# An attention and two-stage MLP kernel: TensorE's order fixed from the second pair's transposes on, and scores of pairs 2 to 4 on four array squares

## The chip, the cores and the metric

The kernel runs on one core of one Trainium2 chip. A core has TensorE (PE; its weight loads are shown as PEld), VectorE (DVE), ScalarE (ACT), GpSimd (POOL) and SyncE (SP), which here issues every DMA. The metric is the time of one execution on the device in microseconds; lower is better.

## What is computed

Attention with a window of 128 keys and a bias that falls with distance, over 4 batches of 8 heads, 576 positions, 64 values a head; then two MLPs on the 2304 tokens.

```python
scores = scale * q @ k.T                       # q, k, v: (4, 8, 576, 64)
scores = where(0 <= i - j < 128, scores + bias, -1e9)
attn   = softmax(scores)
x      = (attn @ v) laid out as (2304, 512)
a, b   = x @ w1, x @ w2                        # 512 -> 1024
x      = (a * b) @ w3 @ w_out                  # 1024 -> 1024 -> 512
h      = x @ w_in                              # 512 -> 2048
out    = (h * clip(h + 3, 0, 6) / 6) @ w_out2  # 2048 -> 512
```

## The kernel before

**Pairs.** Heads are taken two at a time: 16 pairs, four to a batch. `products(n, part)` makes the scores of pair n (tile s, line 159), part 0 for query blocks 0 to 5 and part 1 for 6 to 8. A block has 64 queries against up to 192 keys. The two heads lie in the two halves of the partitions; each matmul uses one 64x64 square of the array. Without a swap only the two squares on the diagonal are used; for pairs above 4 a copy with the halves exchanged (`other`, tiles qo and ko) lets odd blocks use the other two squares. `scores` reduces on DVE (line 173) and takes the exponential on ACT (line 178); `normalize` forms reciprocals on DVE (lines 183 and 184) and scales on POOL (line 187). `pt(n, g)` transposes the probabilities on TensorE (line 214), 24 matmuls for each g, and copies them out on ACT and DVE (tile th, line 220). `pv(n)` multiplies by the values (tile X, line 241) and moves the result out (tile xf, lines 248 and 249), and `x_parts` splits it into x. Each float32 matmul leaves two records in the trace: 24 and 12 for the two parts of the scores, 48 for one pt, 44 for one pv.

**Banks.** All score, transpose and value tiles share three double banks of PSUM, p0 to p2 (`bank2`, line 140): pair n in role r takes p((n+r)%3). So scores of part 1 of pair 1 stand where pv(0) has left its first half, and scores of part 0 of pair 2 where those stood.

**Weights.** w3 and w_out come as 64-bit words. `unpack` makes float32 of them (lines 66, 67, 71), `split` a high and a low part (lines 77 and 78), and `mm3` multiplies in three matmuls (lines 53 to 55). W = w3 @ w_out is made ahead in rows i = 0 to 7 (`w_half(i, half)`, tile wps): rows 0 and 1 in plain float32 (line 393), rows 2 to 7 as two halves of 12 matmuls each. A row needs its `w3_unit(i)`. `more` loads the next raw block into one of three buffers, when that buffer's last user is done. `w12_unit(f)` does the same for w1 and w2.

**Order.** Tile's planner gives each engine a fixed order from its own estimate of times, earlier lines of the program first. `in_order(True, ...)` keeps an instruction behind the one that precedes it in the program on the same engine. Before the first matmul of ab (x times w1 and w2) `written[0]` is false: scores and values stay together but for their first matmul, transposes and `w_half` float. `attn_slot(6n+s)` spreads pair n over six slots, between which `do_work` puts the weight units; `GATE` holds the last halves of W behind pair 3. From the first ab on, `written[0]` is true: `block(k)` puts `gap` pieces of ab or y, 12 matmuls each, between the steps of a pair. Pairs 0 to 3, and the scores of pair 4 (made here in part), come before the first ab; pairs 4 to 7 fill block 0.

**Buffers.** `place(n)` says which of two q, k, v buffers pair n uses: it alternates up to pair 3, after which all use the first. q and k of pair n+2 are loaded behind pt of pair n (`loads`). The exchanged copy had one buffer, in pool a3, which was opened after the raw pools close.

Of the kernel before, what the change touches and what calls it, by code (L numbers as in the profile page):

```python
# [9 lines left out]
F32 = mybir.dt.float32  # L10
# [8 lines left out]
P = 128  # L19
# [4 lines left out]
def tile_attention_moe_moe2(ctx: ExitStack, tc: tile.TileContext, qT, kT, vm, vt, wo, w3, w12, w2x, out):  # L24
# [82 lines left out]
    HB = (slice(0, D), slice(D, 2 * D))  # L107
    qw, kw, vw = [], [], []
    for i, pool in enumerate((a1, a2)):
        qw.append(pool.tile([P, S], F32, name=f"qw{i}"))  # L110
        kw.append(pool.tile([P, S], F32, name=f"kw{i}"))
        vw.append(pool.tile([P, NC, P], F32, name=f"vw{i}"))
# [6 lines left out]
    def load_hp(n, names):  # L119
        for nm in names:  # L120
            if nm == "v":
                nc.sync.dma_start(out=vw[place(n)][:, 0 : NC - 1, :], in_=vm[n])
                nc.sync.dma_start(out=vw[place(n)][D:P, NC - 1, :], in_=vt[n])
            else:
                r, src = (qw, qT) if nm == "q" else (kw, kT)
                nc.sync.dma_start(out=r[place(n)], in_=src[n])
                if n > NP:
                    for h in range(2):
                        nc.sync.dma_start(out=other[nm][HB[h], :], in_=src[n][HB[1 - h], :])

    other = {}
    prob = {}
# [16 lines left out]
    def products(n, part):  # L149

        t = bank2(n, part, f"s_{n}_{part}")
        for a in range(0, len(PARTS[part]), 2):
            for h in range(2):
                for i in PARTS[part][a : a + 2]:
                    swap = n > NP and i % 2 == 1
                    r = 1 - h if swap else h
                    q, k = (other["q"], other["k"]) if swap else (qw[place(n)], kw[place(n)])
                    o = t[:, i % 2, COL[i] : COL[i] + width(i)]
# [140 lines left out]

    def pair_steps(n):  # L300

        if n == NP:
            yield from (lambda s=s: attn_slot(SLOTS * n + s) for s in (2, 3, 4))
        else:

            def first():
                for part in range(2):
                    products(n, part)
                for js in ((0, 1, 2), (3, 4, 5), (6, 7, 8)):
                    scores(n, js)  # L310
                    normalize(n, js)

            def second():
                pt(n, 0)
                loads(n, "q")
                pt(n, 1)
                loads(n, "k")

            yield first
            yield second  # L320
        yield lambda: pv(n)

# [61 lines left out]
    def w_half(i, half):  # L384
# [6 lines left out]
        for m in range(half * KH, (half + 1) * KH):  # L391
            if i < WHOLE:
                nc.tensor.matmul(ps[:, 0:DM], w3v[i][:, m, :], wof[m], start=m == 0, stop=m == KF - 1)
                continue
            hi, lo = w3v[i]
            mm3(ps[:, 0:DM], hi[:, m, :], lo[:, m, :], *wov[m], m == 0, m == KF - 1)
        if half == 1:
# [36 lines left out]

    work = []
    for i in range(KF):
        work += [("w3", i), ("h", i, 0), ("h", i, 1)]
    head = work.index(("w3", 2))
    work[:head] = [
        ("w3", 0), ("wo", 0), ("wo", 1), ("h", 0, 0), ("w3", 1), ("h", 1, 0),  # L440
        ("wo", 2), ("wo", 3), ("h", 0, 1), ("h", 1, 1),
    ]
    a = work.index(("h", WHOLE - 1, 1)) + 1
    work[a:a] = [("ws", i) for i in range(KH)]
    for f in range(W12_EARLY):
        work.insert(work.index(("h", KH + 1 + f, 1)) + 1 if f < KH - 1 else len(work), ("w12", f))
    FILL = {0: 2, 1: 4, 2: 6, 3: 8, 4: 10}
    nslot = SLOTS * NP + 2

    GATE = {  # L450
        (KF - 2, 1): ("pt", NP - 1, 1),
        (KF - 1, 0): ("x", NP - 1, 1), (KF - 1, 1): ("x", NP - 1, 1),
    }

    def do_work(w):
        if w[0] == "h":

            gate = GATE.get(w[1:])
            with tc.issue_after(last_pe[gate].ins) if gate in last_pe else nullcontext():
                w_half(w[1], w[2])  # L460
        else:
# [4 lines left out]
    wi = 0  # L466
    end = work.index(("h", KF - 2, 0))
    for s in range(nslot):
        attn_slot(s)

        upto = FILL[s] if s in FILL else FILL[4] + (s + 1 - len(FILL)) * (end - FILL[4]) // (SLOTS * NP - 2 - len(FILL))
        if s >= SLOTS * NP - 2:
            upto = work.index(("h", KF - 2, 1)) + 1
        if s >= SLOTS * NP:
            upto = len(work)
        while wi < min(upto, len(work)):
            do_work(work[wi])
            wi += 1


    raw_ctx2.close()
    raw_ctx.close()
    a2_ctx.close()
    a3 = apool_ctx.enter_context(tc.tile_pool(name="a3", bufs=1, side="right"))
    for nm in "qk":
        other[nm] = a3.tile([P, S], F32, name=f"{nm}o")
    gp = p1.enter_context(tc.tile_pool(name="gp", bufs=1))
# [169 lines left out]
    def block(k):  # L657

        work = pieces(k)
        for n in range(NP * (k + 1), NP * (k + 2)):  # L660
            steps = list(pair_steps(n))
            gaps = (3, 1, 1, 1) if n == NP else (4, 1, 1) if n == NP + 1 else (3, 1, 1)
            for step, gap in zip(steps, gaps):
                step()
                for _ in range(gap):
                    yield next(work)
# [272 lines left out]
```

## Time and profile before

| | us |
|---|---|
| median of 3 runs | 845.68 (845.66 to 845.82) |
| the profiled execution | 845.8 |
| its span (first to last instruction) | 844.0 |
| TensorE busy | 824.2 |
| DVE, ACT, POOL busy | 466.4, 378.4, 98.1 |
| first matmul of ab starts | 100.47 |

All times on the trace count from the start of the span. A row of the timeline gives start, duration, engine, line, operation, output<-inputs, shapes and a count of merged instructions; in square brackets stands the idle time of the engine before it and what ended it. Matmuls overlap, so the time that a group takes is the distance from its start to the next group's start, not the sum of durations.

### The profile page before, as it was taken

The numbers are of one execution on the slowest core, as the hardware profiler recorded it, in microseconds if no ns is written. First come the engines' busy times: TensorE is split into PE (matmuls) and PEld (weight loads), VectorE is DVE, ScalarE is ACT, GpSimd is POOL, SyncE is SP. The second block draws the span as 40 slices with busy tenths as digits, with TensorE's granted clock in tenths as the row PEclk, the third lists the DMA queues.
The fourth block names the chain that finished last, engine by engine and source line by source line (L and its number), as shares of the span: only waits on it lengthen the run. The fifth ranks groups of instructions, "written<-read, shape, count | busy, mean of one in ns | idle before, by whom it ended". The sixth has DMA issues, their size and how long they took to land.

```text
span 844.0 us, 15817 instructions
## 1 busy us (share of the span) xinstructions
PE 824.2 (98%) x6304; PEld 698.5 (83%) x6304; DVE 466.4 (55%) x1054; ACT 378.4 (45%) x820; POOL 98.1 (12%) x185
## 2 busy tenths in 40 slices
PE   5989999999999999999999999999999999999998
PEld 4567777888888788888899898998889889898886
DVE  5985477425452454246573877885543547443543
ACT  7765565525441445224352654555332335332333
POOL 3333303222231222300000000000000000000000
PEclk9989999999999999999999999999999999999999
DMA  9753543334332332316666589589855377455502
GB/s 352 284 217 100 162 137 102 99 100 114 95 91 73 104 81 62 125 64 237 261 194 239 229 333 363 160 303 390 326 196 215 138 274 293 189 208 203 188 1 75
DMA packets 42841, 155.62 MB, mean 184 GB/s; under 512 B 4880, under 2 KB 20240, under 8 KB 31504
## 3 DMA queue, kind: packets, MB, share of 16 engines
q1 hardware_dynamic: 42768, 154.62, 51.2%
q8 instruction: 49, 0.80, 0.4%
q14 instruction: 24, 0.20, 0.1%
HBM read 118.55 MB, written 36.04 MB: 183 GB/s over the span
## 4 chain that ended last, share of the span: by engine, by line
PE 91%; DVE 4%; ACT 2%; DMA 1%; issue 1%; POOL 0%; SPq 0%; DVEq 0%; POOLq 0%
PE ab L53 8%; PE o L54 8%; PE o L55 8%; PE o L53 8%; PE ab L54 8%; PE ab L55 7%; PE h L53 7%; PE h L54 7%; PE h L55 7%; PE y L53 4%; PE y L54 4%; PE y L55 4%; PE s L159 3%; PE X L241 3%; PE pt L214 3%; DMA raww<-in_w_dram 1%
## 5 line engine op out<-in xcount | busy, mean ns | idle before, releaser
L53 PE MATMUL ab<-x,w12h 128*128 128x512 f32 (+1 forms) x320 | 121.3, 379 | 0.4 <-ACT asb L517 0.4
L54 PE MATMUL ab<-x,w12h 128*128 128x512 f32 (+1 forms) x320 | 118.1, 369 | 0.0
L55 PE MATMUL ab<-x,w12l 128*128 128x512 f32 (+1 forms) x320 | 117.9, 369 | 0.0
L53 PE MATMUL h<-yh,va 128*128 128x384 f32 x336 | 114.1, 340 | 0.2 <-DVE rl L748 0.2
L54 PE MATMUL h<-yl,va 128*128 128x384 f32 x336 | 113.3, 337 | 0.3 <-DVE yl L78 0.3
L55 PE MATMUL h<-yh,va 128*128 128x384 f32 x336 | 113.3, 337 | 0.0
L54 PE MATMUL o<-vo,g 128*128 128x512 f32 x288 | 113.2, 393 | 0.0
L53 PE MATMUL o<-vo,g 128*128 128x512 f32 x288 | 113.1, 393 | 0.0
L55 PE MATMUL o<-vo,g 128*128 128x512 f32 x288 | 87.2, 393 | 0.0
L187 POOL TENSOR_SCALAR pr<-pr,rc 128x192 f32<-128x192 f32 (+1 forms) x144 | 71.9, 519 | 131.5 <-ACT pr L178 79.1
L747 ACT ACTIVATE rl<-c,three 128x384 f32<-128x384 f32 x72 | 44.4, 617 | 79.5 <-DVE c L777 48.4
L53 PEld LDWEIGHTS ab<-x,w12h 128*128 128x128 f32 x320 | 60.4, 189 | 14.3 <-issue 2.0
L178 ACT ACTIVATE pr<-pr,mn 128x192 f32<-128x192 f32 (+1 forms) x144 | 61.3, 427 | 19.8 <-DVE mn L173 19.7
L55 PEld LDWEIGHTS ab<-x,w12l 128*128 128x128 f32 x320 | 60.4, 189 | 10.2
L53 PEld LDWEIGHTS h<-yh,va 128*128 128x128 f32 x336 | 63.1, 188 | 6.7 <-DVE rl L748 3.1
L54 PEld LDWEIGHTS ab<-x,w12h 128*128 128x128 f32 x320 | 60.4, 189 | 9.0
L54 PEld LDWEIGHTS h<-yl,va 128*128 128x128 f32 x336 | 63.1, 188 | 4.2 <-DVE yl L78 0.6
L55 PEld LDWEIGHTS h<-yh,va 128*128 128x128 f32 x336 | 63.1, 188 | 0.0
L55 PEld LDWEIGHTS o<-vo,g 128*128 128x128 f32 x288 | 53.9, 188 | 10.5 <-DVE g L78 0.3
L78 DVE TENSOR_TENSOR g<-rl,g 128x384 fp32r<-128x384 f32 x96 | 53.2, 555 | 16.8 <-ACT g L77 14.3
L53 PEld LDWEIGHTS o<-vo,g 128*128 128x128 f32 x288 | 54.1, 188 | 9.5 <-ACT g L77 0.2
L54 PEld LDWEIGHTS o<-vo,g 128*128 128x128 f32 x288 | 54.1, 188 | 9.3
(95 smaller groups left out, 1371.4 us busy)
## 6 DMA issues: line engine op xcount, KB each, us to landing
va<-vad SPq DMA_DIRECT2D x18, 1792.0 KB, 7.4
vo<-vod SPq DMA_DIRECT2D x18, 1024.0 KB, 9.5
raww<-in_w_dram SPq DMA_DIRECT2D x16, 1024.0 KB, 4.9
rawv<-in_w2x_dram SPq DMA_DIRECT2D x16, 1024.0 KB, 7.4
vad<-va SPq DMA_DIRECT2D x8, 1792.0 KB, 7.3
vod<-vo SPq DMA_DIRECT2D x8, 1024.0 KB, 10.9
yraw<-yT SPq DMA_DIRECT2D x21, 384.0 KB, 9.1
qw<-in_qT_dram SPq DMA_DIRECT2D x16, 288.0 KB, 3.9
```

Source lines behind the costliest of these rows:

```text
L53: in_order(pinned, nc.tensor.matmul(ps, lh, rh, start=first, stop=False, **kw))
L54: in_order(pinned, nc.tensor.matmul(ps, lh, rl, start=False, stop=False, **kw))
L55: in_order(pinned, nc.tensor.matmul(ps, ll, rh, start=False, stop=last, **kw))
L78: lo_eng.tensor_tensor(out=lo, in0=src, in1=f32(hi), op=ALU.subtract)
L159: in_order(written[0] or (a, h, i % 2) != (0, 0, 0), nc.tensor.matmul(o[HB[h], :], q[HB[r], i * D : (i + 1) * D], k[HB[r], (i + 1) * D - w ...
L178: nc.scalar.activation(o, o, AF.Exp, bias=mn[:, i : i + 1], scale=-1.0, accum_out=sm[:, i : i + 1])
L187: nc.gpsimd.tensor_scalar(out=o, in0=o, scalar1=rc[:, i : i + 1], scalar2=1.0, op0=ALU.mult, op1=ALU.mult)
L214: last_pe["pt", n, g] = in_order(written[0], nc.tensor.matmul(t[HB[c], h, o : o + D], prob[n, i][HB[h], (k - i + 2) * D : (k - i + 3) * D] ...
L241: last_pe["x", n, h] = in_order(written[0] or begun, nc.tensor.matmul(X[p][HB[h], a * D : b * D], vw[place(n)][HB[p], k // 2, HB[h]], pts[ ...
L747: nc.scalar.activation(rl, h, AF.Relu, bias=three[:, 0:1], scale=1.0)
```

## The change

- Exchanged copies `other` now exist in both places, in pools a1 and a2, and pool a3 is gone. They are loaded, as four more half-height DMAs for each pair, from pair 2 on instead of from pair 5 on; the scores of pairs 2, 3 and 4 swap their odd blocks as those of later pairs do.
- The slots run only to the end of pair 1's scores; behind them come the four `wo_split` and `w3_unit` 2 and 3, and `written[0]` becomes true there. From there every scores, pt, pv and `w_half` matmul up to ab is kept in program order. `GATE` and the slot schedule of the rest are gone.
- That order, with h(i,b) for half b of row i of W: h(2,0), scores(2,0); then for n = 1, 2, 3: half, pt(n) whole, half, pv(n), half, scores(n+1, 1), and for n below 3 half, scores(n+2, 0). That is twelve halves with a step of a pair between each two. `w3_unit(i+2)` stands ahead of row i, and `w12_unit` 0 to 2 behind rows 5 to 7.
- `normalize` of pair 4's last blocks comes ahead of block 0. In block 0, pair 4's two transposes stand together, and pairs 5 to 7 have two pieces between transposes and values instead of one.

```diff
--- before.py
+++ after.py
@@ -106,7 +106,10 @@
     W = {}
     HB = (slice(0, D), slice(D, 2 * D))
     qw, kw, vw = [], [], []
+    other = {}
     for i, pool in enumerate((a1, a2)):
+        for nm in "qk":
+            other[nm, i] = pool.tile([P, S], F32, name=f"{nm}o{i}")
         qw.append(pool.tile([P, S], F32, name=f"qw{i}"))
         kw.append(pool.tile([P, S], F32, name=f"kw{i}"))
         vw.append(pool.tile([P, NC, P], F32, name=f"vw{i}"))
@@ -124,11 +127,10 @@
             else:
                 r, src = (qw, qT) if nm == "q" else (kw, kT)
                 nc.sync.dma_start(out=r[place(n)], in_=src[n])
-                if n > NP:
+                if n > 1:
                     for h in range(2):
-                        nc.sync.dma_start(out=other[nm][HB[h], :], in_=src[n][HB[1 - h], :])
-
-    other = {}
+                        nc.sync.dma_start(out=other[nm, place(n)][HB[h], :], in_=src[n][HB[1 - h], :])
+
     prob = {}
     stat = {}
     pts = {}
@@ -152,9 +154,9 @@
         for a in range(0, len(PARTS[part]), 2):
             for h in range(2):
                 for i in PARTS[part][a : a + 2]:
-                    swap = n > NP and i % 2 == 1
+                    swap = n > 1 and i % 2 == 1
                     r = 1 - h if swap else h
-                    q, k = (other["q"], other["k"]) if swap else (qw[place(n)], kw[place(n)])
+                    q, k = (other["q", place(n)], other["k", place(n)]) if swap else (qw[place(n)], kw[place(n)])
                     o = t[:, i % 2, COL[i] : COL[i] + width(i)]
                     in_order(written[0] or (a, h, i % 2) != (0, 0, 0), nc.tensor.matmul(
                         o[HB[h], :], q[HB[r], i * D : (i + 1) * D], k[HB[r], (i + 1) * D - width(i) : (i + 1) * D],
@@ -297,28 +299,17 @@
             pt(n, s - 3)
             loads(n, "qk"[s - 3])
 
-    def pair_steps(n):
-
-        if n == NP:
-            yield from (lambda s=s: attn_slot(SLOTS * n + s) for s in (2, 3, 4))
-        else:
-
-            def first():
-                for part in range(2):
-                    products(n, part)
-                for js in ((0, 1, 2), (3, 4, 5), (6, 7, 8)):
-                    scores(n, js)
-                    normalize(n, js)
-
-            def second():
-                pt(n, 0)
-                loads(n, "q")
-                pt(n, 1)
-                loads(n, "k")
-
-            yield first
-            yield second
-        yield lambda: pv(n)
+    def first(n, part):
+        products(n, part)
+        for js in ((6, 7, 8),) if part else ((0, 1, 2), (3, 4, 5)):
+            scores(n, js)
+            normalize(n, js)
+
+    def second(n):
+        pt(n, 0)
+        loads(n, "q")
+        pt(n, 1)
+        loads(n, "k")
 
     flat = lambda t: t.rearrange("p a b -> p (a b)")
     KH = KF // 2
@@ -393,7 +384,7 @@
                 nc.tensor.matmul(ps[:, 0:DM], w3v[i][:, m, :], wof[m], start=m == 0, stop=m == KF - 1)
                 continue
             hi, lo = w3v[i]
-            mm3(ps[:, 0:DM], hi[:, m, :], lo[:, m, :], *wov[m], m == 0, m == KF - 1)
+            mm3(ps[:, 0:DM], hi[:, m, :], lo[:, m, :], *wov[m], m == 0, m == KF - 1, pinned=written[0])
         if half == 1:
             split(W["h"][:, i, :], W["l"][:, i, :], ps[:, 0:DM], nc.vector)
 
@@ -432,58 +423,63 @@
     load_wo(3)
     more()
 
-    work = []
-    for i in range(KF):
-        work += [("w3", i), ("h", i, 0), ("h", i, 1)]
-    head = work.index(("w3", 2))
-    work[:head] = [
+    work = [
         ("w3", 0), ("wo", 0), ("wo", 1), ("h", 0, 0), ("w3", 1), ("h", 1, 0),
         ("wo", 2), ("wo", 3), ("h", 0, 1), ("h", 1, 1),
     ]
-    a = work.index(("h", WHOLE - 1, 1)) + 1
-    work[a:a] = [("ws", i) for i in range(KH)]
-    for f in range(W12_EARLY):
-        work.insert(work.index(("h", KH + 1 + f, 1)) + 1 if f < KH - 1 else len(work), ("w12", f))
     FILL = {0: 2, 1: 4, 2: 6, 3: 8, 4: 10}
-    nslot = SLOTS * NP + 2
-
-    GATE = {
-        (KF - 2, 1): ("pt", NP - 1, 1),
-        (KF - 1, 0): ("x", NP - 1, 1), (KF - 1, 1): ("x", NP - 1, 1),
-    }
 
     def do_work(w):
         if w[0] == "h":
-
-            gate = GATE.get(w[1:])
-            with tc.issue_after(last_pe[gate].ins) if gate in last_pe else nullcontext():
-                w_half(w[1], w[2])
+            w_half(w[1], w[2])
         else:
             {"wo": wo_unit, "ws": wo_split, "w3": w3_unit, "w12": w12_unit}[w[0]](w[1])
             if w[0] in ("w3", "w12"):
                 more()
 
     wi = 0
-    end = work.index(("h", KF - 2, 0))
-    for s in range(nslot):
+    for s in range(SLOTS + 3):
         attn_slot(s)
-
-        upto = FILL[s] if s in FILL else FILL[4] + (s + 1 - len(FILL)) * (end - FILL[4]) // (SLOTS * NP - 2 - len(FILL))
-        if s >= SLOTS * NP - 2:
-            upto = work.index(("h", KF - 2, 1)) + 1
-        if s >= SLOTS * NP:
-            upto = len(work)
-        while wi < min(upto, len(work)):
+        while wi < FILL.get(s, len(work)):
             do_work(work[wi])
             wi += 1
-
+    for i in range(KH):
+        wo_split(i)
+    for i in range(WHOLE, WHOLE + 2):
+        do_work(("w3", i))
+    written[0] = True
+
+    def rows():
+        for i in range(WHOLE, KF):
+            if i + 2 < KF:
+                do_work(("w3", i + 2))
+            for half in range(2):
+                w_half(i, half)
+                if half and i > KH:
+                    do_work(("w12", i - KH - 1))
+                yield
+
+    fill = rows()
+    next(fill)
+    first(2, 0)
+    for n in range(1, NP):
+        next(fill)
+        second(n)
+        next(fill)
+        pv(n)
+        if n + 1 < NP:
+            load_hp(n + 2, "v")
+        next(fill)
+        first(n + 1, 1)
+        if n + 2 <= NP:
+            next(fill)
+            first(n + 2, 0)
+    for _ in fill:
+        pass
 
     raw_ctx2.close()
     raw_ctx.close()
     a2_ctx.close()
-    a3 = apool_ctx.enter_context(tc.tile_pool(name="a3", bufs=1, side="right"))
-    for nm in "qk":
-        other[nm] = a3.tile([P, S], F32, name=f"{nm}o")
     gp = p1.enter_context(tc.tile_pool(name="gp", bufs=1))
     sp = p1.enter_context(tc.tile_pool(name="sp", bufs=1))
 
@@ -658,10 +654,14 @@
 
         work = pieces(k)
         for n in range(NP * (k + 1), NP * (k + 2)):
-            steps = list(pair_steps(n))
-            gaps = (3, 1, 1, 1) if n == NP else (4, 1, 1) if n == NP + 1 else (3, 1, 1)
-            for step, gap in zip(steps, gaps):
-                step()
+            late = k == 0
+            if n > NP:
+                first(n, 0)
+                first(n, 1)
+            gaps = (3, 1, 1) if n == NP else (4, 2, 1) if n == NP + 1 else (3, 1 + late, 1)
+            for step, gap in zip((None, second, pv), gaps):
+                if step:
+                    step(n)
                 for _ in range(gap):
                     yield next(work)
         for w in work:
```

## Rows read from the trace of the kernel before

**Rows 1.** The page: busy time by engine, and the chain that ended last.

```profile
PE 824.2 (98%) x6304; PEld 698.5 (83%) x6304; DVE 466.4 (55%) x1054; ACT 378.4 (45%) x820; POOL 98.1 (12%) x185
...
PE 91%; DVE 4%; ACT 2%; DMA 1%; issue 1%; POOL 0%; SPq 0%; DVEq 0%; POOLq 0%
```

**Rows 2.** Windows, whole stretch: length, busy (instructions) by engine, clock, DMA, GB/s.

```profile
37.20:100.47 63.27, 59.14 (x673) 46.66 (x673) 43.08 (x111) 36.71 (x88) 19.88 (x31) 0.95 0.45 161
```

**Rows 3.** Waits of TensorE in 37 to 63 us: total, times, longest.

```profile
PE pt L214 <- POOL pr L187: 1.8, 2, 1.5
PE X L241 <- DVE th L220: 1.2, 1, 1.2
```

**Rows 4.** Windows as in group 2: before and during the clock's fall.

```profile
50.00:54.50 4.50, 1.44 (x33) 0.79 (x33) 4.05 (x8) 3.47 (x6) 2.75 (x3) 0.99 0.47 193
54.50:61.00 6.50, 6.50 (x32) 4.91 (x33) 5.17 (x18) 4.02 (x11) 1.17 (x1) 0.50 0.48 161
```

**Rows 5.** Timeline of TensorE: scores of one pair on two squares, then on four.

```profile
86.08 1.88 PE L159 MATMUL s<-kw,qw 64*64 64x64 f32 x24 [0.36 <-PE pt L214]
...
99.34 1.20 PE L159 MATMUL s<-kw,qw 64*64 64x192 f32 x12
100.47 0.50 PE L53 MATMUL ab<-x,w12h 128*128 128x512 f32 x1
...
120.92 0.27 PE L159 MATMUL s<-kw,qw 64*64 64x64 f32 x1
...
122.49 0.50 PE L53 MATMUL ab<-x,w12h 128*128 128x512 f32 x1
```

**Rows 6.** Timeline of TensorE: transposes, values and the matmuls behind them.

```profile
116.47 1.58 PE L241 MATMUL X<-th,vw 64*64 64x192 f32 x44
117.98 0.50 PE L53 MATMUL ab<-x,w12h 128*128 128x512 f32 x1
...
134.29 1.63 PE L214 MATMUL pt<-ident,pr 64*64 64x64 f32 x96
135.85 0.50 PE L53 MATMUL ab<-x,w12h 128*128 128x512 f32 x1
```

**Rows 7.** Timeline of TensorE and ACT about the first matmuls of this stage.

```profile
35.58 1.48 PE L241 MATMUL X<-th,vw 64*64 64x192 f32 x37
37.19 0.50 PE L53 MATMUL wps<-wovh,w3h 128*128 128x512 f32 x1
...
33.12 1.19 ACT L66 ACTIVATE raww<-raww 128x1024 f32<-128x1024 f32 x1 [0.43 <-DMA raww<-in_w_dram]
...
39.34 0.64 ACT L248 COPY xf<-X 128x576 f32<-128x576 f32 x1
```

**Rows 8.** Timeline of DVE and POOL between pair 1's last scores and transposes.

```profile
44.34 0.84 DVE L67 TENSOR_SCALAR raww<-raww 128x1024 int32<-128x1024 int32 x1 [0.87 <-DMA raww<-in_w_dram]
...
47.84 0.35 DVE L173 CUSTOM_DVE_ANT_0 pr<-s,rel 128x192 f32<-128x192 f32 x1
...
51.63 2.75 POOL L187 TENSOR_SCALAR pr<-pr,rc 128x192 f32<-128x192 f32 x3 [7.00 <-DVE rc L184]
...
63.72 1.23 POOL L187 TENSOR_SCALAR pr<-pr,rc 128x192 f32<-128x192 f32 x3 [0.79 <-DVE rc L184]
```

**Rows 9.** Timeline of TensorE and DVE: pair 5's values and a copy they awaited.

```profile
139.09 0.54 PE L241 MATMUL X<-th,vw 64*64 64x192 f32 x4 [0.23 <-DVE th L220]
140.70 1.54 PE L241 MATMUL X<-th,vw 64*64 64x192 f32 x40 [1.06 <-DVE th L220]
...
140.09 0.55 DVE L220 COPY th<-pt 128x384 f32<-128x384 f32 x1
```

**Rows 10.** DMA in 16 to 32 us (as group 2), and issues: size, landing.

```profile
16.00:32.00 16.00, 14.00 (x115) 6.50 (x116) 15.90 (x33) 14.06 (x25) 9.49 (x10) 0.97 0.99 405
...
qw<-in_qT_dram SPq DMA_DIRECT2D x16, 288.0 KB, 3.9
...
qo<-in_qT_dram SPq DMA_DIRECT2D x22, 144.0 KB, 3.4
```

## The prediction

> **What bounds the kernel now.** Read first the busy line and the chain: TensorE is busy 98% of the span and carries 91% of the chain [rows 1]. So a microsecond of TensorE time that goes away ahead of the end is a microsecond of the whole, unless a wait takes its place. Read next where TensorE is not at its best. Between the first matmul of W's row 2 at 37.19 us and the first of ab at 100.47 us, 63.3 us pass [rows 5, 7]; there DVE is busy for 43.1 us, ACT for 36.7 and POOL for 19.9 [rows 2], so no other engine fills the stage. The waits show 1.8 us for probabilities scaled on POOL and 1.2 us for a transpose's copy [rows 3], 3.0 us together, and a further 0.36 us ahead of scores [rows 5]. Behind the longest of these, after a stretch in which TensorE was busy 1.44 of 4.5 us, the granted clock is 0.50, the lower level of 1.2 GHz, for 6.5 us [rows 4]. Work done at half speed for 6.5 us costs 3.25 us. Last, read the length of like groups of matmuls: a pair's scores on two squares take 1.88 us (part 0) and 1.13 us (part 1, 99.34 to 100.47), 3.0 us together, and on four squares 1.57 us (120.92 to 122.49) [rows 5].
>
> **The change part by part.** It touches the stage from 37 to 100 us and block 0 behind it. I count the new stage from its parts, then check it against the old.
>
> *The written order.* From pair 1's last scores to ab TensorE now has one queue: twelve halves of W, scores of pairs 2 to 4, transposes and values of pairs 1 to 3, none of which can be overtaken. Twelve three-matmul products between other groups take 2.94 us (117.98 to 120.92: one piece of ab, the same twelve matmuls of 512 columns, drain included) [rows 5, 6]. So the halves take 12 x 2.94 = 35.3 us. Transposes of a pair take 1.56 us (134.29 to 135.85) and values 1.51 us (116.47 to 117.98) [rows 6], three times each 4.7 and 4.5 us. Scores of pairs 2 to 4 take 3 x 1.57 = 4.7 us, and pair 1's last part, still on two squares, 1.1 us [rows 5]. The sum is 50.3 us.
>
> *Its start.* Pair 1's last scores go into the bank that pair 0's values leave. Those end at 37.1, but ACT copied them out only at 39.34 to 39.98 us, and the old kernel filled that time with row 2 of W from 37.19 on [rows 7]. The new order puts these scores ahead of row 2, so TensorE may idle there. The earliest start is 37.1 + 0.64 for the copy and some 0.4 for the two hand-overs, 38.2; the latest that the rows speak for is 40.0. I take 40.0, as ACT's order ahead of it is not changed. Ab would then start at 90.3 us, without a further wait.
>
> *New waits.* In the written order the half behind a transpose is all that covers its copies on ACT and DVE. Block 0 already runs such an order, and there pair 5's values waited 0.23 and 1.06 us, since the second copy came at 140.09 us between weight units on DVE [rows 9]; pair 4's did not [rows 6]. So a wait of this kind costs 0 to 1.3 us for each of three pairs; I take one of them, 1.3 us, which gives 91.6 us. What stands queued behind such a wait is everything to ab. Scaled probabilities get 2.94 + 1 + 2.94, about 7 us of cover between a pair's last scores and its transposes; in the old stage three scalings took 1.23 us on a free POOL and 2.75 us at worst [rows 8], which that covers when DVE comes in time.
>
> *The check from the old side.* Of 63.3 us go the waits of 3.0 and 0.36, the clock's 3.25, and 3 x (3.0 - 1.57) = 4.3 us of scores: 10.9, which leaves 52.4. A gap of 40.0 - 37.2 = 2.8 us at the start and a wait of 1.3 us come in: 56.5, so ab starts at 93.7 us. The two counts give 91.6 and 93.7 us; their middle, 92.7 us, is 7.8 us before the old 100.47.
>
> *Block 0.* Pairs 5 to 7 have two pieces between transposes and values instead of one, 5.9 us in place of 2.94, so the 1.3 us that pair 5's values waited [rows 9] go. Pair 4's transposes stand together; this saves one change of form, between 0 and 0.3 us, counted at nothing. The piece taken for this comes from the tail of the same block: no work is added.
>
> *Loads.* Each of pairs 2, 3 and 4 brings four more DMAs of 144 KB, 0.59 MB, and SP issues all in order. For pairs 3 and 4 they stand beside loads of weights that are wanted some 15 us later in the new order than in the old: nothing. Pair 2's fall into 16 to 32 us, where the DMA engines are 0.99 busy at 405 GB/s [rows 10]: what is queued behind them, row 4 of w3, comes 0.59 MB / 405 GB/s = 1.5 us later. If a half-height load is slower by the byte, as its landing of 3.4 us for 144 KB beside 3.9 us for 288 KB [rows 10] would have it, 1.7 times as much, 2.5 us. Row 4 is wanted at about 57 us in the new order, so I count nothing; but ACT already waited 0.43 us for it at 33.12 [rows 7], and what ACT has queued behind is the copying that frees TensorE's banks. So this can cost 0 to 2.5 us at the start; I take 0 and keep the rest for a rival.
>
> *DVE, ACT and POOL* do the same operations as before, 43.1 us of DVE in a stage that shrinks to 55.5 us: a share of 78% instead of 68%. That is the load that it had in 50 to 61 us (9.2 of 11 us) or a little under [rows 4], and there it was late.
>
> *Sum.* The gain is 7.8 + 1.3 = 9.1 us. The profiled execution took 845.8 us with a span of 844.0, and agrees with the median of 845.68 to 0.1. Behind block 0 nothing is anchored to a fixed time; all moves forward. 845.7 - 9.1 = 836.6 us.
>
> **The rivals.**
>
> *A, the vector chain holds the order up once.* In the old stage DVE took pair 1's last score blocks only at 47.84 us, behind an unpacking of w3 that waited 0.87 us for its DMA at 44.34 [rows 8]; its order is planned with estimated times. If it does so again, scores of pair 2, which need that bank, stand until 48.7 where TensorE could start them at 40.0 + 1.1 + 2.9 = 44.0: 4.7 us. Then 1.0 for them, 2.9 for a half and 0.8 for half the transposes bring TensorE to 53.4, and the rest waits for POOL until 54.4 (51.63 + 2.75) [rows 8]: 1.0 us more. If the clock falls again, 3.25 us [rows 4]. Together 9.0: 845.6 us. Without the clock, and with half of the delay, 839.5. For it speaks that only the TensorE order is written, not DVE's; against it, that pair 1's scores now come ahead of row 2, so that the planner sees them ready earlier.
>
> *B, slower: the same at every pair.* Where the old order let TensorE take any ready half of W while it waited, the new one cannot. If DVE is late for pairs 2 and 3 as well, by the 1.3 us of the copies each [rows 9], A's 845.6 becomes 848.2 us. It decides from 9.1 us of new idle time on, and its place is the stage from 40 to 60 us. Against it speaks that DVE's weight work after 60 us is sparser: POOL's scalings are back at 1.23 us [rows 8].
>
> The Trainium skill ("SBUF — State Buffer", "SBUF: two separate sides") says that POOL and a DVE operation with two SBUF inputs hold a shared port in turn, each for its whole length, which speaks against packing both closer. The trace agrees in that the three scalings went from 1.23 to 2.75 us; by the rule they would be at 2.75 at every pair, which the 7 us of cover still hold, so that it only raises B.
>
> *C, the early queue.* Pair 2's four loads push ACT back as above: 2.5 us, 839.1 us. The row for it is the DMA share of 0.99; against it, that the half-height loads are issued behind the weights that are wanted first.
>
> *D, the swap brings nothing there.* Its 4.3 us stay: 840.9 us. The 1.57 us of pair 5 [rows 5] speak against it.
>
> **How the numbers follow.** Forecast 836.6 us, chance 0.60, with an own range of 832 to 840: down by a start at 38.2 (1.8) and no copy wait (1.3) and by the first count alone (1.0), up by two more copy waits (2.6). C 0.08, D 0.04. A 0.18, of which 0.05 within 0.2% of before (1.7 us; about what a measurement of this kernel can tell from no change). B 0.10. The range of 8 in 10 reaches from 831.5 to 843.0, over C, D and the lower half of A; above lie B and the rest of A, 0.17. Faster: 0.60 + 0.08 + 0.04 + 0.13 = 0.85; same 0.05; slower 0.10.
>
> **What would show it.** Right: ab's first matmul at 89 to 95 us, each pair's scores of 2 to 4 in 1.6 to 1.8 us with qo and ko among their inputs, no granted clock of 0.5 after 45 us, no wait for th in block 0. Wrong: scores of pair 2 that wait for DVE past 45 us (A, B), an ACT wait for raww of over 1.5 us at about 33 us (C), a long gap ahead of pair 1's last scores beyond 40 us, or waits of ab in block 0 for weight units that the shorter stage has left for later.

## The result, and the profile after

The changed kernel takes 852.13 us (851.32 to 852.28) where the kernel before, beside it, takes 845.75: a ratio of 1.0072, 95% interval 1.0055 to 1.009. The prediction, 836.6 us and faster, was wrong in sign. The profiled execution took 852.12 us, with a span of 850.3. Most lines of this stage lie two higher than before: scores 161, transposes 216, values 243, copies th 222 and xf 250; raw loads went from 343 to 334.

The page after: busy time by engine, and the chain that ended last (before: [rows 1]).

```profile
PE 821.6 (97%) x6304; PEld 694.6 (82%) x6304; DVE 465.9 (55%) x1054; ACT 378.0 (44%) x820; POOL 97.7 (11%) x185
...
PE 88%; DMA 5%; DVE 3%; ACT 2%; issue 1%; SPq 0%; DVEq 0%; ACTq 0%
```

TensorE is busy 2.6 us less, yet the span is 6.3 us longer: the matmuls got shorter, as meant, and idle time came in. The chain shows where from: DMA went from 1% to 5%. TensorE's waits after, first in 36 to 63 us, then in 63 to 109 us (total, times, longest), against 1.8 and 1.2 us in [rows 3]:

```profile
PE X L243 <- DVE th L222: 5.3, 2, 4.8
PE s L161 <- ACT xf L250: 4.7, 1, 4.7
...
PE X L243 <- DVE th L222: 4.3, 1, 4.3
```

The same three waits on TensorE's timeline, each in its square bracket, and the first matmul of ab, at 108.81 us instead of 100.47 [rows 5]:

```profile
41.43 2.12 PE L161 MATMUL s<-kw,qw 64*64 64x192 f32 x12 [4.67 <-ACT xf L250]
...
61.48 2.83 PE L243 MATMUL X<-th,vw 64*64 64x192 f32 x40 [4.85 <-DVE th L222]
...
84.33 3.29 PE L243 MATMUL X<-th,vw 64*64 64x192 f32 x44 [4.27 <-DVE th L222]
...
108.81 0.50 PE L53 MATMUL ab<-x,w12h 128*128 128x512 f32 x1
```

The groups behind the waits are long too: 2.12 us for scores that take 1.1 [rows 5], 3.29 for values that take 1.5 [rows 6]. The windows say why (columns as in [rows 2]; the clock stands behind POOL's column). Behind each of these three idle stretches the granted clock is at 0.64 to 0.70 in the mean; in the windows after that it is 1.00 again:

```profile
41.43:47.10 5.67, 5.67 (x24) 3.93 (x25) 5.41 (x11) 4.61 (x10) 1.86 (x1) 0.70 0.96 315
...
61.48:68.13 6.65, 6.65 (x61) 5.32 (x62) 3.75 (x4) 2.83 (x5) 1.31 (x1) 0.70 0.28 87
68.13:80.06 11.93, 11.93 (x167) 8.91 (x158) 5.01 (x25) 6.23 (x22) 2.29 (x6) 1.00 0.64 189
84.33:91.34 7.01, 7.01 (x57) 5.73 (x57) 1.10 (x2) 1.39 (x3) 1.31 (x1) 0.64 0.17 42
91.34:108.81 17.47, 17.47 (x237) 13.30 (x237) 9.66 (x33) 9.80 (x28) 5.16 (x10) 1.00 0.15 51
```

What stood ahead of the late copies is on the timelines of ACT (pair 0's values, xf) and DVE (transposes, th):

```profile
39.69 1.17 ACT L66 ACTIVATE raww<-raww 128x1024 f32<-128x1024 f32 x1 [1.50 <-DMA raww<-in_w_dram]
40.73 0.65 ACT L250 COPY xf<-X 128x576 f32<-128x576 f32 x1
...
60.27 0.70 DVE L67 TENSOR_SCALAR raww<-raww 128x1024 int32<-128x1024 int32 x1 [2.28 <-DMA raww<-in_w_dram]
60.87 0.55 DVE L222 COPY th<-pt 128x384 f32<-128x384 f32 x1
...
79.96 0.70 DVE L67 TENSOR_SCALAR raww<-raww 128x1024 int32<-128x1024 int32 x1 [5.17 <-DMA raww<-in_w_dram]
...
83.72 1.01 DVE L222 COPY th<-pt 128x384 f32<-128x384 f32 x2
```

Each time the engine stood idle for a raw weight block that had not landed (1.50, 2.28 and 5.17 us), with a copy that TensorE needed queued behind the unpacking of that block. The first is row 4 of w3; the other two are blocks of w1 and w2, which nobody wants before ab. SP's timeline shows why row 4 came late: it was issued at 33.40 us, behind the exchanged halves of pair 3; before, it was the first of three issues from 22.78 us on (first row, from the kernel before; the rest is after):

```profile
22.78 16.98 SPq L343 DMA_DIRECT2D raww<-in_w_dram  x3
...
27.86 1.14 SPq L132 DMA_DIRECT2D qo<-in_qT_dram  x2
29.05 3.31 SPq L132 DMA_DIRECT2D ko<-in_kT_dram  x2
33.40 0.33 SPq L334 DMA_DIRECT2D raww<-in_w_dram  x1
```

### The profile page after: what moved, and what is told of

The parts are those of the page before. It is cut to its first block, busy times and chain, and to the rows that moved or that the text cites. A ratio compares the mean times of both kernels' runs of the same rounds, so it can differ in the third digit from the quotient of the medians.

```text
span 850.3 us, 15838 instructions
## 1 busy us (share of the span) xinstructions
PE 821.6 (97%) x6304; PEld 694.6 (82%) x6304; DVE 465.9 (55%) x1054; ACT 378.0 (44%) x820; POOL 97.7 (11%) x185
## 4 chain that ended last, share of the span: by engine, by line
PE 88%; DMA 5%; DVE 3%; ACT 2%; issue 1%; SPq 0%; DVEq 0%; ACTq 0%
PE o L54 8%; PE o L55 8%; PE o L53 8%; PE ab L53 8%; PE ab L54 7%; PE ab L55 7%; PE h L53 7%; PE h L54 7%; PE h L55 7%; DMA raww<-in_w_dram 4%; PE y L53 4%; PE y L54 4%; PE y L55 4%; PE X L243 3%; PE s L161 2%; PE pt L216 2%
```

## The experiments

All times are medians of runs beside the kernel before, which stood at 845.7 to 846.8 us in these comparisons; ratios are to it, with 95% intervals. The theory: two losses, each a wait of ACT or DVE for weights in front of a copy, one made by the exchanged loads and one by where the planner put the unpacking of w1 and w2; the halves of the change are sound. The rival: the written order itself, or the swap, costs the time. The edits are shown in part; where the early exchanged loads are left out, those of pair 5 are also kept in program order on SP.

**The two halves of the change, each alone.** Order without swap and loads; swap and loads in the old order; and everything changed but with TensorE left free until block 0.

```diff
 # order alone: after, with
-                if n > 1:
+                if n > NP:
-                    swap = n > 1 and i % 2 == 1
+                    swap = n > NP and i % 2 == 1
 # swap alone: before, with other in a1 and a2, and
-                if n > NP:
+                if n > 1:
-                    swap = n > NP and i % 2 == 1
+                    swap = n > 1 and i % 2 == 1
 # order free: after, without
-    written[0] = True
```

> The kernel after, but the scores of pairs 2 to 4 stay on two squares and their exchanged copies are not loaded (pair 5's are loaded in their place in the queue). TensorE's written order is kept. Two theories for the 8.3 us by which ab starts later in the kernel after (108.8 against 100.5 us). Loads: the added half-height loads stand on SP ahead of the raw weights (row 4 of w3 was issued at 33.4 us instead of 22.8), the weights land late, and ACT and DVE, which unpack them in order, hold up TensorE. Vector order: TensorE's order lets it overtake nothing, and DVE's planned order puts the unpacking of w1/w2 blocks ahead of the copies of transposes; that stalls with or without the loads. By loads the three waits (4.7, 4.9 and 4.3 us) and the low clock behind them go and 4.3 us of slower scores come back: 838 to 843 us. By vector order only the first wait goes, which the scores eat up: 849 to 853 us.

> The kernel before, with the exchanged copies loaded and used for pairs 2 to 4, and its own slots, gates and free order of TensorE. By loads the late weights of w3 cost several us here too: 846 to 851 us. By vector order TensorE can overtake, the loads are hidden, and the scores save 3 x 1.4 = 4.3 us: 840 to 843 us.

> The kernel after with its program order, loads and swap, but TensorE is not held to that order until block 0: transposes and halves of W may be moved by the planner. If the fixed order itself is the harm, TensorE fills the waits with halves of W: 841 to 845 us. If late weights and the unpacking on DVE are, little changes, as in the kernel before with the swap alone (850.6): 847 to 853 us.

Measured: order alone 848.83 us, 1.0033 (1.0011 to 1.0056); swap alone 850.57 us, 1.0044 (1.003 to 1.0058); order free 849.03 us, 1.0025 (1.0011 to 1.0038). Each half loses by itself, and 0.33 and 0.44% add up to about the 0.72% of both. That fits two losses rather than one; the rest of the runs take them apart. With TensorE left free 0.47 of the 0.72% goes and 0.25% stays: the fixed order lays the waits bare, but doesn't make all of the loss.

**Undoing each suspected cause in the changed kernel.** The three early blocks of w1 and w2 unpacked in program order (late); the exchanged loads kept in program order on SP (in place); both.

```diff
 # late unpacking
-            {"wo": wo_unit, "ws": wo_split, "w3": w3_unit, "w12": w12_unit}[w[0]](w[1])
+            if w[0] == "w12":
+                w12_unit(w[1], True)
+            else:
+                {"wo": wo_unit, "ws": wo_split, "w3": w3_unit}[w[0]](w[1])
 # loads in place
-    nc.sync.dma_start(out=other[nm, place(n)][HB[h], :], in_=src[n][HB[1 - h], :])
+    in_order(n <= NP, nc.sync.dma_start(out=other[nm, place(n)][HB[h], :], in_=src[n][HB[1 - h], :]))
```

> The kernel after, with the unpacking of the three early w1/w2 blocks kept in program order on ACT and DVE, that is behind the copies of transposes and of W's rows that precede it. Loads unchanged. By vector order the second and third wait (4.9 and 4.3 us) and the clock's falls behind them go: 839 to 843 us, ab at 96 to 99 us. By loads the first wait stays and weights still land late: 848 to 852 us.

> The kernel after, with the half-height loads kept in program order on SP: pair 3's no longer go ahead of row 4 of w3 but wait behind pair 3's own q and k. By loads this takes away the first wait and brings the weights earlier: 838 to 845 us. By vector order only the first wait goes (4.7 us, less if TensorE then waits later): 847 to 850 us.

> The kernel after with both edits tried singly before: half-height loads in program order on SP, and the three early w1/w2 blocks unpacked in program order. If late weights and the place of the unpacking are the two causes and add up, the waits for copies of transposes go with the low clock, and what is left is the wait for pair 0's values (3 us): ab at 93 to 97 us, 838 to 842 us. If TensorE's fixed order stalls on something else as soon as one wait goes, ab stays at 99 to 101 us: 843 to 847 us.

> The kernel after without the swap and its loads for pairs 2 to 4 (as e1_order_alone), with the three early w1/w2 blocks unpacked in program order. By vector order the two waits of 4.8 us each for copies go: ab at 94 to 97 us, 838 to 843 us; the scores are 4.3 us slower than with the swap. By loads nothing is left to gain here: 846 to 849 us.

Measured: late unpacking 847.0 us, 1.001 (0.9996 to 1.0024); loads in place 846.27, 1.0006 (0.9995 to 1.0017); both 843.82, 0.9967 (0.9955 to 0.9979); order alone with late unpacking 844.51, 0.9971 (0.9962 to 0.9981). Against the 1.0072 of the change, each mending gives 0.6 to 0.7% back, and both together make it faster than the kernel before. Yet none of the four came down to the range that its expectation gave for the theory. The waits in 36 to 109 us, first of late unpacking, then of loads in place, show what each took away:

```profile
PE s L161 <- ACT xf L250: 4.4, 1, 4.4
PE X L243 <- DVE th L222: 2.4, 2, 1.9
```

```profile
PE s L161 <- ACT xf L250: 4.0, 2, 3.0
PE pt L216 <- POOL pr L189: 1.7, 2, 0.9
PE s L161 <- issue: 1.5, 1, 1.5
PE pt L216 <- issue: 1.5, 1, 1.5
PE X L243 <- DVE th L222: 0.6, 1, 0.6
```

Late unpacking brings the waits for th from 9.6 to 2.4 us and leaves the wait for xf at 4.4. Loads in place shortens the wait for pair 0's copy to 3.0 us, and the waits for th fall to 0.6 although the unpacking is left to the planner; 4.7 us of other waits come in. So the two causes don't stand behind one wait each: the long waits for th took both an unpacking ahead of the copy and a block that lands late. In order alone, without any early exchanged loads, waits for th of 5.6 us are left. Each trace is of one execution, here of 845.42 and 844.19 us, both below their medians.

In order alone with late unpacking, a wait for xf of 3.4 us is the only one left in that stretch. So the written order itself does not cost the time: with the unpacking kept in program order it gains 0.29%.

**The copy ahead of the unpacking.** ACT still unpacked rows of w3 ahead of pair 0's copy. The first edit puts row units 4 to 7 behind that copy; the second, instead, only behind pair 1's scores on DVE and exponentials on ACT.

```diff
 # copy first: both mended, and
-                do_work(("w3", i + 2))
+                with tc.issue_after(xf_copy[0].ins):
+                    do_work(("w3", i + 2))
 # weights behind: the same place, instead
+                with tc.issue_after(score[1].ins), tc.issue_after(power[1].ins):
```

> As e5_both_mended, and ACT's unpacking of row 4 of w3 is queued behind the copy of pair 0's values, for which pair 1's last scores wait. If that wait (4.7 us in the kernel after, 3.0 with the loads in place) is only ACT waiting in order for a late weight, 2 us more go than in e5_both_mended: 836 to 840 us, ab at 91 to 95 us. If the copy is late for another reason, no difference to e5_both_mended.

> As e9_copy_first, but rows 4 to 7 of w3 are unpacked, on ACT and on DVE, behind pair 1's last scores and exponentials. In e9_copy_first TensorE still waits 2.3 us for the bank of these scores and 2.2 us for their probabilities. If both are DVE taking the weights first, up to 4.5 us more go: 838 to 840 us, ab at 91 to 93 us. If the weights' own unpacking then comes too late or crowds the next pair, no gain: 842 to 844 us.

Copy first: 842.18 us, 0.9956 (0.9945 to 0.9967), ab from 95.85 us; it beats both kernels. Its copy stands at 37.04 us on ACT, ahead of the next unpacking, and the scores follow at once:

```profile
37.04 0.64 ACT L251 COPY xf<-X 128x576 f32<-128x576 f32 x1
...
37.73 1.20 PE L162 MATMUL s<-kw,qw 64*64 64x192 f32 x12 [0.54 <-ACT xf L251]
...
44.17 0.30 PE L162 MATMUL s<-kw,qw 64*64 64x64 f32 x2 [2.27 <-issue]
...
51.80 1.25 PE L217 MATMUL pt<-ident,pr 64*64 64x64 f32 x36 [2.20 <-POOL pr L190]
```

So the earliest start of the prediction, 38.2 us, was there to be had. The 2.27 and 2.20 us in the last two rows are most of what is left; the granted clock is 1.00 from 36 to 96 us. The trace names no cause for the 2.27. But DVE has read pair 1's last scores, which stand in the same bank, only at 43.99 us, behind an unpacking at 41.41 that waited 0.93 us for its load; that is the bank of which rival A spoke, and the two waits are 4.5 us against its 5.7 without the clock. Weights behind was meant to take that away and gave 846.18 us, 0.9998 (0.9987 to 1.0009), worse than either of its ranges: the weight work then stands in front of the next steps (ACT waited 3.70 us for a block at 58.27, with pair 1's copy behind it), and waits of 2.6 (probabilities), 2.1 (xf) and 2.2 us (nothing named) take its place.

**What the exchanged loads cost.** The loads of pairs 2 to 4 made in the old order, with no swap until pair 5, so that nothing reads them; the same loads with 16 of 576 columns; and the swap in the old order with its loads in place. In loads alone and tiny loads, and in loads alone at full height below, the exchanged loads of pairs 4 and 5 are kept in program order on SP.

```diff
 # loads alone: swap alone, but
-                    swap = n > 1 and i % 2 == 1
+                    swap = n > NP and i % 2 == 1
 # tiny loads: loads alone, but
+                        w = S if n > NP else 16
-    ... out=other[nm, place(n)][HB[h], :], in_=src[n][HB[1 - h], :]
+    ... out=other[nm, place(n)][HB[h], 0:w], in_=src[n][HB[1 - h], 0:w]
 # swap, loads in place: swap alone, and in_order(n <= NP, ...) around the load
```

> The kernel before with the half-height loads of pairs 2 to 4 as in e2_swap_alone, but the scores of these pairs stay on two squares: the loads are made for nothing. If the swap is worth its 4.3 us and the loads cost the rest of what e2_swap_alone lost, 853 to 855 us. If the swap is worth nothing there, about 850 us as e2_swap_alone.

> As e12_loads_alone with the same DMAs in the same places on SP, but each moves only 16 of 576 columns; the scores of pairs 2 to 4 stay on two squares. If the cost of the loads is SP's queue standing behind them (each waits for a place, and row 4 of w3 is issued at 33 us), it costs as much as e12_loads_alone. If the cost is their bytes on the DMA engines, it is the kernel before: 845 to 847 us.

> The kernel before with the swap as in e2_swap_alone, and the half-height loads kept in program order on SP, so that pair 3's no longer go ahead of row 4 of w3. If going ahead was what the loads cost, the swap's gain shows: 842 to 845 us. If any load of that size in this stage costs, 847 to 850 us.

Loads alone: 851.03 us, 1.0056 (1.0034 to 1.0077). Tiny loads: 846.51, 1.0004 (0.9995 to 1.0014). So it is the transfer that costs, some 4.5 us, and not SP's four more instructions a pair. Row 4's place on SP isn't what counts here: tiny loads too issue row 4 only from 31.00 us on.

```profile
31.00 9.93 SPq L346 DMA_DIRECT2D raww<-in_w_dram  x3
```

In the old order one of the waits that the loads make is rival A's. In loads alone, pair 2's first scores waited 2.73 us until 52.02; DVE had read pair 1's last ones, in the same bank, up to 51.92, behind an unpacking at 48.65 that waited 0.83 us for its load. Tiny loads have no such wait. With loads in place the swap alone stands at 848.37, 1.003 (1.0014 to 1.0047): in the old order it still loses.

**Bytes, or height?** The exchanged copy in one load of 128 partitions: q and k lie in memory with their second half repeated ahead of the first. The bytes moved are the same.

```diff
-                nc.sync.dma_start(out=r[place(n)], in_=src[n])
+                nc.sync.dma_start(out=r[place(n)], in_=src[n][D : 3 * D])
-                    for h in range(2):
-                        nc.sync.dma_start(out=other[nm, place(n)][HB[h], :], in_=src[n][HB[1 - h], :])
+                    nc.sync.dma_start(out=other[nm, place(n)], in_=src[n][0 : 2 * D])
```

> The kernel before, with exchanged loads of pairs 2 to 4 made for nothing (no swap until pair 5), as in the run with the loads alone, but each exchanged copy comes in one load of 128 partitions: q and k lie in memory with their second half repeated ahead of the first. The bytes are the same 0.59 MB a pair. If the loads cost by their bytes, the time stays at about 851 us (ratio 1.005 to 1.007). If they cost by the half height, the DMA rate in 24 to 32 us goes back to about 400 GB/s, row 4 of w3 lands before 37 us, and the time is 846 to 848.5 us (ratio 1.0005 to 1.003).

> The changed kernel with exchanged copies in one load of 128 partitions each, nothing else. By half height: TensorE's wait for pair 0's copy goes from 4.7 us to 1 to 3 us, the unpacking of w1 and w2 still holds the transposes' copies; 847 to 850.5 us (ratio 1.0015 to 1.0055). By bytes: 852 us as before (ratio 1.006 to 1.009).

> The swap for pairs 2 to 4 alone in the order of the kernel before, exchanged copies in one load of 128 partitions each. By half height: 843 to 848 us (ratio 0.997 to 1.002), since the cost of the loads falls away and up to 4.3 us of scores are saved. By bytes: about 850.5 us as with half-height loads (ratio 1.003 to 1.006).

> The version with both parts mended and pair 0's copy ahead of the unpacking, with exchanged copies in one load of 128 partitions each. By half height: what is left ahead of ab shrinks by 0 to 3 us, and the time is 838 to 842 us (ratio 0.991 to 0.9955). By bytes: no change against that version, 842 to 843 us (ratio 0.9955 to 0.997).

Windows of loads alone, first with half-height loads, then in one load (the last three columns are clock, DMA share and GB/s):

```profile
24.00:28.00 4.00, 4.00 (x19) 1.66 (x18) 3.90 (x7) 2.82 (x4) 4.00 (x4) 1.00 1.04 261
28.00:32.00 4.00, 4.00 (x55) 2.20 (x54) 2.71 (x4) 2.52 (x3) 1.41 (x3) 1.00 0.99 322
```

```profile
24.00:28.00 4.00, 4.00 (x42) 1.81 (x46) 3.90 (x5) 3.25 (x4) 4.00 (x4) 1.00 1.03 403
28.00:32.00 4.00, 4.00 (x38) 1.74 (x30) 3.32 (x5) 3.12 (x4) 0.63 (x2) 1.00 1.04 407
```

At the same full share the engines move 261 to 322 GB/s with half-height loads among them and 403 to 407 without: the rate hangs on how the same bytes are loaded. In the changed kernel that moves row 4's issue from 33.40 to 27.67 us, and the time falls to 845.69 us, 0.9994 (0.9979 to 1.001): the whole loss is gone. Late unpacking took nearly as much back, so the two don't add up. One of the two blocks for which DVE waited was itself queued behind exchanged loads (that of 79.96 us was issued at 71.83, behind pair 4's); the other, that of 60.27, was issued at 52.55, when row 5's split on DVE, which ended at 52.52, had freed its buffer. With full height one wait for th is left, of 2.3 us. Swap alone falls to 848.0, 1.0017 (1.0006 to 1.0028). Loads alone did not follow: 850.3 us, 1.0044 (1.0029 to 1.0059), although SP issues row 4 at 28.73 instead of 35.73 us; by its expectation that speaks for the bytes. Pair 2's wait has shrunk from 2.73 to 0.78 us there, but another stands in its place (first row on TensorE, the others on DVE):

```profile
74.97 0.45 PE L160 MATMUL s<-kw,qw 64*64 64x64 f32 x6 [3.38 <-issue]
...
68.70 0.88 DVE L67 TENSOR_SCALAR raww<-raww 128x1024 int32<-128x1024 int32 x1 [0.91 <-DMA raww<-in_w_dram]
...
74.52 0.34 DVE L174 CUSTOM_DVE_ANT_0 pr<-s,rel 128x192 f32<-128x192 f32 x1
```

These are pair 3's first scores, and the trace names nothing that they wait for. By `bank2` they stand in the bank of pair 2's last scores (both p0), and DVE read these only up to 74.87 us, behind the unpacking of a block of w1 and w2 that had waited 0.91 us for its load. It is rival A's wait again, one pair later; no run tries that reading by itself. In the mended version full height gives 842.27 us, 0.9944 (0.9929 to 0.9959), not to be told from 0.9956, which fits that with row 4 ahead of them these loads hold up nobody.

**What the swap is worth in the written order, and whether full height and late unpacking are enough.** Copy first without the swap and its loads for pairs 2 to 4; the changed kernel with full-height loads and late unpacking, loads left to the planner.

```diff
 # order mended, no swap: copy first, but
-                if n > 1:
+                if n > NP:
-                    swap = n > 1 and i % 2 == 1
+                    swap = n > NP and i % 2 == 1
 # full height and late unpacking: the edits shown above, together
```

> The written order without the swap and its loads for pairs 2 to 4, with the late unpacking of w1 and w2 and with pair 0's copy ahead of the unpacking of w3's rows 4 to 7. If the swap is worth what the prediction gave it in the written order (4.3 us, less 0 to 2 us for the loads), this stands 2 to 4 us behind the version with both parts: 844 to 846.5 us (ratio 0.997 to 1.000). If the loads eat the swap's gain, as in the free order, the two are alike: 841 to 843 us (ratio 0.994 to 0.9965).

> The changed kernel with full-height exchanged loads, left to the planner's place, and with the late unpacking of w1 and w2. If the two losses are apart, the 2.3 us that the values of a pair waited for a transpose's copy go, and the time is 842 to 844.5 us (ratio 0.9945 to 0.9985). If the loads' place in SP's queue must be mended as well, the wait for pair 0's copy and the second such wait stay or grow: 845 to 847 us (ratio 0.999 to 1.0015).

Without the swap 844.53 us, 0.9977 (0.9968 to 0.9987), ab from 99.55 us. With it ab starts 3.7 us sooner, of which 0.21% of the time, 1.8 us, is left at the end; the two were run in different comparisons, and their intervals only just part. Full height and late unpacking: 843.49, 0.9964 (0.995 to 0.9978); its waits in 36 to 109 us:

```profile
PE s L160 <- ACT xf L249: 3.3, 1, 3.3
PE pt L215 <- POOL pr L188: 1.4, 2, 1.0
PE X L242 <- DVE th L221: 0.5, 1, 0.5
```

The waits for th are down to 0.5 us and the one for xf is still 3.3, as where the unpacking alone was mended (4.4) and as in the order without the loads (3.4). Full height keeps the loads from making it worse; of the edits tried, only the order on ACT removes it.

## Why the prediction was wrong, point by point

**What bounds the kernel**: right. TensorE carries 88% of the chain, and what moved was its idle time ahead of ab.

**The sum of the groups**: nearly right. A step of scores and the half behind it take 3.75 us (91.34 to 95.09, part 1 of a pair) and 3.98 (95.09 to 99.07, part 0), which less 2.94 each is 1.85 us for a pair where 1.57 was counted: 0.8 us for three. The swap took place, with qo and ko among the inputs:

```profile
91.34 0.37 PE L161 MATMUL s<-kw,qw 64*64 64x192 f32 x1
...
95.09 0.27 PE L161 MATMUL s<-kw,qw 64*64 64x64 f32 x1
95.10 0.32 PE L161 MATMUL s<-ko,qo 64*64 64x128 f32 x1
...
99.07 1.63 PE L216 MATMUL pt<-ident,pr 64*64 64x64 f32 x96
```

**The start**: 41.43 instead of 40.0 us, 1.4 late. The prediction took it from ACT's order, as not changed. Row 4's unpacking does stand ahead of copy xf in both kernels. But before, it began at 33.12 us, long ahead of the copy at 39.34 [rows 7]; now it waited 1.50 us for its load until 39.69, and the copy came right behind it at 40.73. It was the landing that moved.

**New waits, the term that failed.** The sum had one wait for th of 1.3 us; there were 0.43, 4.85 and 4.27, 9.55 together. The bound of 1.3 came from block 0 [rows 9], where a copy was late behind weight units whose data had landed. Here the copy stood behind a unit that itself waited for a DMA, so that the bound had to include the landing. Late unpacking took 7 us of these waits away, and loads in place 9, so both the place of the unpacking and the landing belong to the cause.

**The clock**: counted at no loss; in the three windows above it costs 5.67 x 0.30 + 6.65 x 0.30 + 7.01 x 0.36 = 6.2 us. Each of these three waits was followed by a fall of its own; the single fall of [rows 4] should have been priced with each.

Added up: 41.43 + 50.3 + 0.8 + 9.55 + 6.2 = 108.3 us; ab started at 108.81.

**Loads**: the second step that failed. They were counted at nothing for pairs 3 and 4, as standing beside weights that are wanted later. But a load into a fresh buffer depends on nothing, and the planner put pair 3's exchanged halves ahead of row 4 on SP. The 0 to 2.5 us at the start were for pair 2 alone; half-height loads were put at 1.7 times the time by the byte, where the windows, with other loads among them, show 1.3 to 1.5 times, but the term it went into was set to 0. In the changed kernel the loads' form and place are worth 5.6 (loads in place) to 6.6 us (full height), through the same waits and clock as above; in the old order loads alone cost 4.5 us.

The Trainium skill ("SBUF — State Buffer", "Door 1: The DMA port swizzle (why `[64,N]` ≈ `[32,N]`)") says that a transfer to 64 partitions reaches half of the memory's ports, and in "Can I just issue two DMAs to hit both halves?" that two such transfers do not add up. The 261 to 322 GB/s beside 403 to 407 agree with both in direction; no window here holds half-height loads alone.

**Block 0**: right. ab started 8.3 us later and the span grew by 6.3, so 2.0 us came back behind it; 1.3 were foreseen, and its waits for th are gone. Where the other 0.7 us came from is not shown.

**The check from the old side** fell with the same two terms; two counts that share a missing wait agree for no reason. Two of its readings were also a little short: 0.51 us of the old stage's waits, at 83.25 us, were not taken in, and three scalings took 3.10 us at 59.84, so 2.75 was not the worst.

**The rivals.** B, slower because DVE is late at several pairs, had the right mechanism in its copies, with a chance of 0.10 and a price of 2.6 us for two pairs; it was 9.1 for two, and the clock on top. It also built on A, which did not happen in the changed kernel, so that its 848.2 us came near the result by other terms. C had the right queue, but with pair 2's loads instead of pair 3's, and only 1.4 us of it at the start. D was wrong in the written order, where the swap is worth about 1.8 us of its 4.3, and right in the old one, where its loads cost more than it gives. A's waits are what is left in the best version, 2.3 and 2.2 us, and its wait for the bank stands in the old order with the loads.

What stays open: whether DVE's late reading is all that holds the scores in loads alone at full height, which no run tried, and whether the 2.3 and 2.2 us of the best version can go without crowding the next steps.

## What to carry to other kernels

When one engine's order is fixed, every engine that feeds it needs its own queue read for what stands ahead of the needed copy, and for which DMA that in turn waits; a wait is priced with the landing behind it and with the clock's fall after it. A load that depends on nothing may be moved ahead of loads that are wanted first, so pin it behind them. Exchange halves in memory and load all 128 partitions at once, rather than by two loads of 64; that was worth 0.78% in the changed kernel, and nothing clear once the loads were pinned.

## What the runs showed of the hardware

Two half-height loads beside others took a DMA share of 0.99 to 1.04 at 261 to 322 GB/s; the share alone doesn't tell that the engines move little. And three idle stretches of 4.27 to 4.85 us of TensorE were each followed by a mean granted clock of 0.64 to 0.70, of the two levels of 1.2 and 2.4 GHz, over 5.7 to 7.0 us; a wait of 4.6 us in the mean thus cost about 6.7.
